# A gated mix of windowed attention and a GLU on one core: copies moved behind exponentials, three edits to the start

## The chip, the cores and the metric

The kernel runs on one core of one Trainium2 chip. The metric is the device time of one execution in microseconds, as the median of several runs, compared between the kernel before and the kernel after the change.

## The reference

Everything is float32, for one sequence of 2048 tokens with 512 features. Branch A is attention with 32 heads of 16 features, where each query sees itself and the 255 keys before it. Branch B is a gated linear unit with 1376 hidden features. A sigmoid gate for each token mixes them.

```python
g = sigmoid((x * gate_w).sum(-1, keepdims=True))
# A: qkv = x @ wqkv; scores = q k^T * 16**-0.5, masked to 0 <= i - j < 256; softmax; @ v; @ wo
# B: h = sigmoid(x @ w_gate) * (x @ w_up); h @ w_down
return g * a + (1 - g) * b
```

## The kernel before

Precision. TensorE is fed with a reduced 32-bit type. Each operand of a projection is therefore kept as two parts: a high part, made by a cast on ScalarE, and a low part, the difference from the original, made on VectorE (`lower`, `split`). A product is three matmuls: high times high, high times low, low times high.

Order. Apart from GpSimd, every engine's instruction order is the order in which the Python code issues the instructions (line 83). An engine that waits for something holds up all that stands behind it on the same engine.

The start. After fourteen warm-up matmuls on a cleared tile (lines 213 to 221) the loop at line 226 loads, for each of the four blocks d of 128 input features, the value weights and the first 512 tokens of x, both on SyncE's queue. ScalarE casts the weights and x, VectorE makes the low parts. For the first block alone, x is cast in two halves of 256 tokens: the first half by VectorE, the second by ScalarE. The matmuls that use them are those of lines 564 to 573 (`vps`): four token blocks, each in a bank of PSUM, over the four d. For the first d they run half by half, for the others all four token blocks together.

The long stretch. Attention runs over NU = 128 units u, one for each group of four heads (8 groups) and block of 128 tokens (16 blocks), with four heads hh in a unit. One pass of the inner loop, a slot, issues the scores of unit u for the maxima (`s_part`, line 372, TensorE and then a reduction on VectorE) and the transposed scores of unit u - 9 with their exponential (`st_part`, line 440; the exponential is line 454, on ScalarE). Both have two banks of PSUM each. Every eight units, at a wide visit, the products with v are taken (`pv_wide`).

The fill. Behind each slot the generator `turns` issues matmuls of the gate and up projections and of later query and key projections. How many steps follow a slot is written out in GAPS2 (first cycle) and GAPS3 (all others): lists of 31 sizes for the 32 slots of a cycle of eight units, the slot before a visit having none. A step is a pair of matmuls, one on each half of TensorE's rows. Three groups of 12 steps (for each half) share three banks. When a group is complete its copy out of PSUM, `gu_post` (line 633) or `proj_raw` (line 307), both on ScalarE, is put on the list `evac`.

Where a copy is issued. From line 1012: if u lies in the long stretch (`long`, from unit 9 to unit 120) and the slot is not the last one before a visit, a pending copy is issued ahead of the slot's scores, and so ahead of its exponential on ScalarE (`early`). Outside that stretch it is issued behind them (line 1035). Casts for later weights (`acts`, line 1037) are issued behind the scores too, when no copy was. Low parts and the like, on VectorE, come from the list `behind`.

The place of a slot in its cycle is k8 = (u - 9) % 8 * 4 + hh, from 0 to 31. The gap in front of it is GAPS3[k8 - 1]. GAPS3 has the value 2 at 1, 2, 4, 8 to 10, 21 to 23 and 28 to 30, the value 6 at 0, and 3 elsewhere.

Of the kernel before, what the change touches and what calls it, by code (L numbers as in the profile page):

```python
# [7 lines left out]
F32 = mybir.dt.float32  # L8
# [6 lines left out]
P = 128  # L15
# [6 lines left out]
HG = 4  # L22
# [18 lines left out]
LAG = 9  # L41
PVLAG = LAG + 4
WIDE = 2 * 4
# [6 lines left out]
GAPS3 = [6, 2, 2, 3, 2] + GAPS2[5:]  # L50
# [19 lines left out]
def gated_mix_kernel(  # L70
# [11 lines left out]
    nc = tc.nc  # L82
# [42 lines left out]
    NU = NG * NB  # L125
# [22 lines left out]
    with ExitStack() as actx:  # L148
# [45 lines left out]
        wvraw = Vf[:, 0:ND * D].rearrange("p (d n) -> p d n", d=ND)  # L194
# [3 lines left out]
        wv_v = wv.rearrange("(c p) n -> p c n", p=P)  # L198
# [12 lines left out]
            return dst, fill_d[v:v + 1].partition_broadcast(8).rearrange("(a j) o f -> a j (o f)", j=2)  # L211

        warm = cpool.tile([P, CH2], F32R, tag="hb", name="warm", bufs=2)
        nc.vector.memset(warm[:, 0:2 * P].bitcast(F32), 0.0)
        warm_ps = ps.tile([P, CH], F32, tag="st", name="warm_ps", bufs=2)

        def idle_mm(n):
# [5 lines left out]
        def lower(lo, src, hi):  # L223
            nc.vector.tensor_tensor(lo, src, hi.bitcast(F32), op=ALU.subtract)

        for d in range(ND):
            nc.sync.dma_start(wvraw[:, d], wv_v[:, d])
            nc.sync.dma_start(xraw[:, 0, d], xT[0, d])
            nc.scalar.copy(wvh[:, d], wvraw[:, d])
            if d:  # L230
                lower(wvl[:, d], wvraw[:, d], wvh[:, d])
            for h in range(2) if d == 0 else (None,):
                ts = slice(0, CH) if h is None else slice(h * CH // 2, (h + 1) * CH // 2)
                (nc.vector.tensor_copy if h == 0 else nc.scalar.copy)(xh[:, d, ts], xraw[:, 0, d, ts])
                if h == 0:
                    lower(wvl[:, 0], wvraw[:, 0], wvh[:, 0])
                lower(xl[:, d, ts], xraw[:, 0, d, ts], xh[:, d, ts])
        raw_q = [load_wqk(g) for g in range(2)]
# [115 lines left out]
        def run_dmas(dmas):  # L354
            for dst, src in dmas:
                nc.sync.dma_start(dst, src)
# [48 lines left out]
        def max_store(s):  # L405
            nc.sync.dma_start(max_d[s].rearrange("a h l b t -> (a h l b) t"), nms.pop(s))
# [66 lines left out]
        evac = []  # L473
# [89 lines left out]
              for b, (t, n) in enumerate((("s", 2), ("s", 2), ("st", 2), ("misc", 3)))]  # L563
        for d in range(ND):
            for w, bb in (
                [(w, (2 * h, 2 * h + 1)) for h in range(2) for w in range(3)] if d == 0
                else [(w, range(4)) for w in range(3)] if d < ND - 1 else [(None, range(4))]
            ):
                for b in bb:
                    bs = slice(b * P, (b + 1) * P)  # L570
                    for v in range(3) if w is None else (w,):
                        mm(vq[b], (xl if v == 2 else xh)[:, d, bs], (wvl if v == 1 else wvh)[:, d],  # L572
                           start=d == 0 and v == 0, stop=d == ND - 1 and v == 2)
# [51 lines left out]
        def gu_mm(f, c, w, k, half=None, second=False):  # L625
            if (f, c, w) not in gp:
                assert (f, w) in ready, (f, c, w)
                gp[f, c, w] = ps.tile([P, CH], F32, tag="misc", name=f"gu{f}_{c}_{w}", bufs=3)
            return group_mm(gp[f, c, w], gv[:, 0, w], gv[:, 1, w], c, k, half, second)
# [89 lines left out]
        def proj_slot(s, k, half):  # L719
            g, c = divmod(s, NC)  # L720
            d, w = divmod(k, 2) if k < 2 * ND else (k - 2 * ND, 2)
            r = slice(64 * half, 64 * half + 64)
            mm(pair_of_banks(f"ph{s}")[half], wq[g][int(w == 2)][r, d], (xl if w == 1 else xh)[r, d, c * CH:(c + 1) * CH],
               start=k == 0, stop=k == 3 * ND - 1)

        def proj_sum(s):
            lower, upper = halves.pop(f"ph{s}")
            t = cpool.tile([P, CH], F32, tag="sp", name=f"psum{s}", bufs=5)
            nc.scalar.copy(t, lower)
            pj[s] = t  # L730
            behind.append(lambda: nc.vector.tensor_tensor(t, upper, t, op=ALU.add))
            soon.append(lambda: proj_post(s))
# [6 lines left out]
                lambda k, h=None, x=False, a=(f, c, w): gu_mm(*a, k, h, x),  # L739
# [68 lines left out]
        def flush(acts):  # L808
            while acts:
                acts.pop(0)()  # L810
# [92 lines left out]
        def mid(u):  # L903
            return PVLAG <= u < NU and (u - PVLAG) % 4 == 0 and u not in visits

        U_WIDE = NB * NWIDE + LAG
        visits = {u: 2 for u in range(PVLAG + 4, U_WIDE + 1, WIDE)}
# [6 lines left out]
        for u in range(N):  # L914
# [48 lines left out]
            for s4 in proj_at.get(u, ()):  # L963
                if u < LAG:
                    first.insert(0, (
                        lambda k, h, s4=s4: proj_slot(s4, k, h), lambda s4=s4: proj_sum(s4)))
# [4 lines left out]
            for hh in range(HG):  # L971
                wide = visits.get(u) == 2
                if hh == 0 and u in visits:
                    s2 = (u - PVLAG) // 4 - wide
                    if wide:
                        banks = [[pv], []]
                        for n, tag in ((0, "st"), (1, "st"), (1, "s")):
                            banks[n].append(ps.tile([P, CH], F32, tag=tag, name=f"pv{s2}_{tag}{n}", bufs=2))
                        pv_wide(s2, banks)
                    else:  # L980
                        pv_part(s2, pv)
                if hh == 3 and mid(u + 1):
                    max_split((u - 4) // 4)
                if hh == 0 and mark:
                    if not mid(u):
                        max_split((u - 5) // 4)
                    run_dmas(later)
                    later.clear()
                    max_store((u - 5) // 4)
                if hh == 0 and wide:  # L990
                    flush(evac)
                    ripe = [held.pop(0) for _ in range(2) if held and held[0] // 2 == u // 8 + 1]
                    for s4 in ripe:
                        proj_hi(s4)
                    max_load((u - 5) // 4)
                    for s4 in ripe:
                        proj_lo(s4)
                    run_dmas(later)
                    later.clear()
                    for guests, n in ((acts, 2), (behind, 2 - len(ripe))):  # L1000
                        for _ in range(min(n, len(guests))):
                            guests.pop(0)()
                    o_sum(s2, 0, banks[0])
                    if behind:
                        behind.pop(0)()
                    o_sum(s2, 1, banks[1])
                    o_store(s2)
                elif hh == 0 and u in visits:
                    evac.append(lambda s2=s2: o_take(s2, pv))
                if hh == 2 and mark:  # L1010
                    transfers()
                long = LAG <= u < U_WIDE
                early = long and len(evac) > 0 and (hh < HG - 1 or u + 1 not in visits)
                if early:
                    evac.pop(0)()
                pair = [lambda: s_part(u, hh)] if u < NU else []
                if 0 <= u - LAG < NU:
                    pair.append(lambda: st_part(u - LAG, hh ^ 1 if u < NU else hh))
                for part in pair[::-1] if u % NB < 2 else pair:
                    part()  # L1020
                if u < LAG:
                    flush(behind)
                    if hh % 2 == 1:
                        upto = n_first * (2 * u + 1 + hh // 2) // (2 * LAG)
                        run_first(upto - done)
                        done = upto
                else:
                    k8 = (u - LAG) % WIDE * HG + hh
                    dense = GAPS2[max(0, k8 - 1)] < 3 if long else u < NU and (u - PVLAG) % 4 == 3 and hh > 0
                    k = (u - PVLAG) % 4 * HG + hh  # L1030
                    free = hh == 2 and not mid(u + 1) if long else k in (1, 5, 9) or k in (3, 7) and len(behind) > 2
                    guest = behind and (u < PVLAG or u >= NU or free)
                    if guest:
                        behind.pop(0)()
                    if evac and not long and not (u < NU and (guest or hh == 3 and mid(u + 1))):
                        evac.pop(0)()
                    elif acts and not early and not dense and (u < NU or hh % 2 == 1):
                        acts.pop(0)()
                if u >= LAG and (hh % 2 == 1 or u < NU) and (u + 1 not in visits or hh < HG - 1):
                    if u < N - 2:  # L1040
                        next(slots)
# [207 lines left out]
```

## Time and profile before

| | |
|---|---|
| median of three runs | 712.52 us (711.7 to 712.6) |
| the profiled execution | 711.69 us |
| its span, first to last instruction | 710.0 us |
| TensorE matmul busy | 705.3 us, 7542 matmuls |
| VectorE busy | 495.2 us |
| ScalarE busy | 435.3 us |
| GpSimd busy | 171.9 us |

The profile is of one execution. Times are in microseconds from the start of the span. A row of a view in order of time merges instructions of one kind that follow one another on their engine: the first number is the start of the first, the second the time to the end of the last, the number behind the x how many there are. In brackets stand the engine's idle time before the row and what ended it. PE is TensorE's matmuls, PEld its weight loads, DVE is VectorE, ACT ScalarE, POOL GpSimd, SP SyncE; a q behind the name is the engine's sequencer. The ends of matmuls are modelled, so distances between starts are the better measure of TensorE's pace.

### The profile page before, as it was taken

What the parts mean: (1) busy time and instruction counts of PE and PEld (TensorE: products, weight loads), DVE (VectorE), ACT (ScalarE), POOL (GpSimd) and SP (SyncE); (2) the same over time, 40 slices, a digit from 0 to 9 for tenths busy, and PEclk for the clock granted to TensorE, in tenths of its full rate; (3) what the DMA queues carried; (4) which work ended last, traced back from release to release, by engine and by line L of the source; (5) the groups of instructions that cost most, each with busy time, mean ns of one, the idle gap of its engine ahead of it and who ended that gap; (6) DMA issues with size and microseconds to landing.
All of it is one profiled execution on the core that took longest, in us unless ns stands there. A gap on an engine that the chain in (4) does not pass through costs nothing.

```text
span 710.0 us, 20054 instructions
## 1 busy us (share of the span) xinstructions
PE 705.3 (99%) x7542; PEld 626.6 (88%) x7542; DVE 495.2 (70%) x1484; ACT 435.3 (61%) x889; POOL 171.9 (24%) x254
## 2 busy tenths in 40 slices
PE   9999999999999999999999999999999999999998
PEld 7888889999899998999889989999888888888886
DVE  5368767767777776776777777777747858667481
ACT  6423777677676677767767767765676735435341
POOL 5200333233233233323323323333341000000000
PEclk9999999999999999999999999999999999999999
DMA  8466644636446264573645627664579859778521
GB/s 307 115 196 195 216 162 145 218 126 210 155 168 229 79 231 157 164 226 114 200 152 186 213 80 214 209 210 112 179 202 289 268 141 244 168 187 241 149 62 60
DMA packets 102832, 127.38 MB, mean 179 GB/s; under 512 B 45750, under 2 KB 62390, under 8 KB 102736
## 3 DMA queue, kind: packets, MB, share of 16 engines
q1 hardware_dynamic: 102592, 125.98, 58.0%
q8 instruction: 59, 0.97, 0.6%
q14 instruction: 37, 0.30, 0.1%
q10 hardware_dynamic: 144, 0.13, 0.1%
HBM read 71.80 MB, written 51.13 MB: 173 GB/s over the span
## 4 chain that ended last, share of the span: by engine, by line
PE 99%; DVE 0%; issue 0%; DVEq 0%
PE gu L294 28%; PE pj L294 13%; PE st L447 6%; PE s L382 6%; PE tp L673 6%; PE pd L100 5%; PE pd L98 5%; PE pd L99 5%; PE pv_st L502 4%; PE vh L710 4%; PE pv_s L502 3%; PE pa L98 2%; PE pa L99 2%; PE pa L100 2%; PE pv L502 2%; PE vps L572 2%
## 5 line engine op out<-in xcount | busy, mean ns | idle before, releaser
L388 DVE CUSTOM_DVE_ANT_0 junk<-s,mask 128x384 f32<-128x384 f32 (+2 forms) x512 | 271.3, 530 | 93.0 <-PE s L382 39.7
L294 PE MATMUL gu<-xh,w 64*128 64x512 f32 x1152 | 270.8, 392 | 0.0
L454 ACT ACTIVATE pbuf<-st 128x384 f32<-128x384 f32 (+2 forms) x344 | 164.3, 490 | 59.7 <-PE st L447 26.5
L294 PE MATMUL gu<-xl,w 64*128 64x512 f32 x576 | 186.1, 389 | 0.0
L447 PE MATMUL st<-ring 64*128 64x384 f32 (+2 forms) x536 | 167.0, 328 | 0.0
L382 PE MATMUL s<-ring 64*128 64x384 f32 (+2 forms) x536 | 163.9, 324 | 0.1
L294 PEld LDWEIGHTS gu<-xh,w 64*128 64x128 f32 x1152 | 159.7, 184 | 4.0
L461 POOL TENSOR_SCALAR_AFFINE_SELECT pbuf<-pbuf 128x512 f32<-128x512 f32 x86 | 58.1, 676 | 276.1 <-ACT pbuf L454 266.9
L382 PEld LDWEIGHTS s<-ring 64*128 64x128 f32 x536 | 94.9, 184 | 10.7 <-DVE mx L388 2.6
L447 PEld LDWEIGHTS st<-ring 64*128 64x128 f32 x536 | 95.7, 184 | 8.2 <-ACT V L454 2.1
L294 PEld LDWEIGHTS gu<-xl,w 64*128 64x128 f32 x576 | 92.0, 184 | 1.2
L454 ACT ACTIVATE V<-st 128x384 f32<-128x384 f32 (+2 forms) x168 | 72.5, 440 | 29.9 <-PE s L382 17.8
L294 PE MATMUL pj<-xl,wqh 64*128 64x512 f32 (+1 forms) x228 | 80.5, 389 | 0.0
L294 PE MATMUL pj<-xh,wqh 64*128 64x512 f32 (+1 forms) x228 | 80.3, 389 | 0.0
L294 PE MATMUL pj<-xh,wql 64*128 64x512 f32 (+1 forms) x228 | 69.7, 389 | 0.0
L99 PE MATMUL pd<-ring,hb 128*128 128x512 f32 x160 | 62.3, 389 | 0.0
L98 PE MATMUL pd<-ring,hb 128*128 128x512 f32 x160 | 62.3, 389 | 0.0
L100 PE MATMUL pd<-ring,hb 128*128 128x512 f32 x160 | 62.3, 389 | 0.0
L94 ACT CAST hb<-V 128x512 fp32r<-128x512 f32 x40 | 24.9, 622 | 60.1 <-DVE V L873 46.5
L467 POOL TENSOR_SCALAR_AFFINE_SELECT pbuf<-pbuf 128x512 f32<-128x512 f32 x84 | 56.0, 666 | 0.0
L633 ACT COPY sp<-gu 128x512 f32<-128x512 f32 x72 | 42.3, 587 | 13.7 <-PE gu L294 8.9
L461 POOL TENSOR_SCALAR_AFFINE_SELECT V<-V 128x512 f32<-128x512 f32 x42 | 28.0, 667 | 71.2 <-ACT V L454 50.1
(155 smaller groups left out, 1372.1 us busy)
## 6 DMA issues: line engine op xcount, KB each, us to landing
gu_scratch<-sp SPq DMA_DIRECT2D x72, 256.0 KB
V<-gu_scratch SPq DMA_DIRECT2D x36, 512.0 KB
ring<-stack_scratch SPq DMA_DIRECT2D x56, 256.0 KB
stack_scratch<-sh SPq DMA_DIRECT2D x14, 512.0 KB
stack_scratch<-sl SPq DMA_DIRECT2D x14, 512.0 KB
ring<-stack_scratch SPq DMA_DIRECT2D x14, 512.0 KB
guraw<-in_wgu_dram SPq DMA_DIRECT2D x18, 256.0 KB
v_scratch<-V SPq DMA_DIRECT2D x4, 1088.0 KB
```

The costliest lines, as they stand in the source:

```text
L98: mm(ps, lh, rh, start=first, stop=False)
L99: mm(ps, lh, rl, start=False, stop=False)
L100: mm(ps, ll, rh, start=False, stop=last)
L294: return mm(pt, (wl if w == 2 else wh)[r, d], (xl if w == 1 else xh)[r, d, c * CH:(c + 1) * CH], start=k == 0 and not second, stop=k == 3 ...
L382: mm(pt[:, (k - k0) * P:(e - k0) * P], lhsT, blk(g, k, hh, 1, e - k), start=k == k0, stop=e == i + 1, skip_group_check=True,)
L388: nc.vector.tensor_tensor_reduce(junk[:, 0:n], pt[:, 0:n], mask[:, 3 * P - n:], scale=1.0, scalar=NEG, op0=ALU.add, op1=ALU.max, accum_out ...
L447: mm(pt[:, (q - j) * P:(e - j) * P], lhsT, blk(g, q, hh, 0, e - q), start=q == j, stop=e == last, skip_group_check=True,)
L454: exps.append(nc.scalar.activation(out, pt[:, 0:n * P].rearrange(seen, t=HB, **({} if len(out.shape) == 3 else {"k": 2})), AF.Exp, scale=S ...
L461: nc.gpsimd.affine_select(buf[:, s0:s0 + 2], buf[:, s0:s0 + 2], pattern=[[HB, 2], [0, HG], [1, HB]], compare_op=ALU.is_ge, fill=0.0, base= ...
L467: nc.gpsimd.affine_select(old, old, pattern=[[-HB, 2], [0, HG], [-1, HB]], compare_op=ALU.is_gt, fill=0.0, base=0, channel_multiplier=1,)
L502: mm(bank[32 * hh:32 * hh + w, o + k * HB:o + e * HB], vt[HB * half:HB * half + HB, v:v + w], p_run(g * NB + j, hh, half, k, e), start=fir ...
L673: return mm(tp[b][:, 0:TW], (xl if w == 1 else xh)[r, d, b * P:(b + 1) * P], tw[d][int(w == 2)][r, 0:TW], start=k == 0 and not second, sto ...
```

## The change

Four things are altered.

- The zeros for the warm-up matmuls: VectorE clears the first 128 of the 256 columns and GpSimd the others.
- The first block of the value weights is loaded by a DMA that is issued on ScalarE's queue; all other loads stay on SyncE's.
- The second block of x (d = 1) is also cast in two halves, the first by VectorE and the second by ScalarE, and its matmuls run half by half like those of the first.
- In the long stretch a pending copy is issued behind the slot's scores and exponential, and no longer ahead of them, where k8 is over 8 and the gap in front of the slot has fewer than three steps (`tight`). The test that no copy is issued in the last slot before a visit now holds for the stretch behind as well.

```diff
         warm = cpool.tile([P, CH2], F32R, tag="hb", name="warm", bufs=2)
-        nc.vector.memset(warm[:, 0:2 * P].bitcast(F32), 0.0)
+        nc.vector.memset(warm[:, 0:P].bitcast(F32), 0.0)
+        nc.gpsimd.memset(warm[:, P:2 * P].bitcast(F32), 0.0)
...
         for d in range(ND):
-            nc.sync.dma_start(wvraw[:, d], wv_v[:, d])
+            (nc.sync if d else nc.scalar).dma_start(wvraw[:, d], wv_v[:, d])
             nc.sync.dma_start(xraw[:, 0, d], xT[0, d])
...
-            for h in range(2) if d == 0 else (None,):
+            for h in range(2) if d < 2 else (None,):
...
-                if h == 0:
+                if h == 0 and d == 0:
                     lower(wvl[:, 0], wvraw[:, 0], wvh[:, 0])
...
-                [(w, (2 * h, 2 * h + 1)) for h in range(2) for w in range(3)] if d == 0
+                [(w, (2 * h, 2 * h + 1)) for h in range(2) for w in range(3)] if d < 2
...
                 long = LAG <= u < U_WIDE
-                early = long and len(evac) > 0 and (hh < HG - 1 or u + 1 not in visits)
+                k8 = (u - LAG) % WIDE * HG + hh
+                tight = long and k8 > 8 and GAPS3[k8 - 1] < 3
+                last = hh == HG - 1 and u + 1 in visits
+                early = long and len(evac) > 0 and not last and not tight
...
-                    if evac and not long and not (u < NU and (guest or hh == 3 and mid(u + 1))):
+                    if evac and not last and (tight if long else not (u < NU and (guest or hh == 3 and mid(u + 1)))):
                         evac.pop(0)()
```

## Rows read from the trace of the kernel before

**Rows 1.** The page: its first line, and TensorE's busy time, share and instructions.

```profile
span 710.0 us, 20054 instructions
PE   705.3 (99%) x7542; PEld 626.6 (88%) x7542; DVE 495.2 (70%) x1484; ACT 435.3 (61%) x889; POOL 171.9 (24%) x254
```

**Rows 2.** All waits of TensorE's matmuls: us in total, times, longest.

```profile
PE warm_ps L219 <- DVE warm L214: 1.3, 1, 1.3
```

**Rows 3.** In order of time, the first 9 us, all engines (columns as described above).

```profile
0.80 0.42 POOL L247 MEMSET mask<- 128x384 f32 x1 [0.29 <-POOLq L1236]
0.81 0.39 SPq L227 DMA_DIRECT2D V<-in_wv_dram  x1
0.93 0.27 DVE L214 MEMSET warm<- 128x256 f32 x1 [0.93 <-PEq L1236]
...
1.25 3.36 PE L219 MATMUL warm_ps<-warm 128*128 128x256 f32 x14 [1.25 <-DVE warm L214]
1.26 0.41 SPq L228 DMA_DIRECT2D V<-in_xT_dram  x1
...
3.44 0.62 ACT L229 CAST w<-V 128x512 fp32r<-128x512 f32 x1 [1.36 <-DMA V<-in_wv_dram]
...
4.08 0.41 ACT L234 CAST xh<-V 128x256 fp32r<-128x256 f32 x1
4.08 0.29 DVE L234 CAST xh<-V 128x256 fp32r<-128x256 f32 x1 [2.89 <-DMA V<-in_xT_dram]
...
4.50 0.50 PEld L572 LDWEIGHTS vps<-w,xh 128*128 128x128 f32 x2 [0.18 <-ACT xh L234]
...
4.90 0.75 DVE L224 TENSOR_TENSOR xl<-V,xh 128x256 fp32r<-128x256 f32 x2
...
6.94 0.62 ACT L234 CAST xh<-V 128x512 fp32r<-128x512 f32 x1 [1.38 <-DMA V<-in_xT_dram]
...
7.19 0.62 PE L572 MATMUL vps<-w,xl 128*128 128x512 f32 x2
...
7.61 0.76 PEld L572 LDWEIGHTS vps<-w,xh 128*128 128x128 f32 x4 [0.23 <-ACT xh L234]
7.64 1.17 PE L572 MATMUL vps<-w,xh 128*128 128x512 f32 x4
...
8.65 1.08 PE L572 MATMUL vps<-wvl,xh 128*128 128x512 f32 x4
```

**Rows 4.** In order of time, the last microseconds: the one DMA on ScalarE's queue.

```profile
707.20 0.37 ACTq L1197 DMA_DIRECT2D out_dram<-spare  x1
```

**Rows 5.** In order of time, TensorE's matmuls around a copy at k8 = 11.

```profile
106.95 0.33 PE L447 MATMUL st<-ring 64*128 64x384 f32 x1
...
108.68 0.33 PE L447 MATMUL st<-ring 64*128 64x384 f32 x1
...
108.86 0.39 PE L294 MATMUL gu<-xh,w 64*128 64x512 f32 x1
```

**Rows 6.** In order of time, ScalarE at the same place.

```profile
106.80 0.49 ACT L454 ACTIVATE pbuf<-st 128x384 f32<-128x384 f32 x1 [0.15 <-PE st L447]
107.31 0.59 ACT L633 COPY sp<-gu 128x512 f32<-128x512 f32 x1
107.79 1.06 ACT L454 ACTIVATE pbuf<-st 128x384 f32<-128x384 f32 x2
```

**Rows 7.** Waits of TensorE's weight loads from 73 to 485 us: total, times, longest.

```profile
PEld st L447 <- ACT V L454: 2.1, 7, 0.3
...
PEld st L447 <- ACT pbuf L454: 1.4, 5, 0.3
```

**Rows 8.** In order of time: two of these 12 waits, and ScalarE at the second.

```profile
93.03 0.18 PEld L447 LDWEIGHTS st<-ring 64*128 64x128 f32 x1 [0.33 <-ACT V L454]
...
443.24 0.18 PEld L447 LDWEIGHTS st<-ring 64*128 64x128 f32 x1 [0.27 <-ACT V L454]
...
443.26 0.59 ACT L633 COPY sp<-gu 128x512 f32<-128x512 f32 x1
```

More of the change, by code (lines that the diff above doesn't have):

```diff
@@ L1027, in gated_mix_kernel @@
                 else:
-                    k8 = (u - LAG) % WIDE * HG + hh
                     dense = GAPS2[max(0, k8 - 1)] < 3 if long else u < NU and (u - PVLAG) % 4 == 3 and hh > 0
```

## The prediction

> **What bounds the kernel now.** I read the page first: TensorE is busy for 705.3 of the 710.0 us of the span [rows 1]. That alone does not prove that it is the bound, since the ends of matmuls are modelled, so the list of TensorE's waits came next: in the whole run it holds a single one, 1.3 us before the first warm-up matmul [rows 2]. From there to the last output matmul one matmul follows another. So an edit pays only if it shortens that stream: by letting real matmuls start earlier, or by removing a gap between two of them. A copy or a cast that merely moves on another engine pays nothing. The views to read are therefore the first 9 us in order of time (what the first matmuls wait for) and the waits of the weight loads in the long attention stretch (what opens gaps there). The profiled execution took 711.69 us, 0.83 us below the median of the three runs (712.52); the sum is made against 711.69 and the same difference is applied to the median.
>
> **Zeros cleared by two engines.** VectorE clears 256 columns in 0.27 us (from 0.93), and the warm-up matmuls start at 1.25, 0.05 us after it [rows 3]. Half of that is 0.13 us. GpSimd clears 384 columns in 0.42 us from 0.80 [rows 3], so its 128 columns, which now stand ahead of the mask, take about 0.14 and are done by 0.95, before VectorE is. The warm-up starts and ends 0.13 us earlier. That is worth nothing by itself, because the first real weight load already waits 0.18 us beyond the warm-up [rows 3]: it only raises the possible gain at that place to 0.31. GpSimd's later work slips 0.14 us; none of it releases TensorE here.
>
> **First weights on ScalarE's queue.** Today SyncE issues the weights at 0.81 and x at 1.26; the casts show them landed at 3.44 and 4.08 [rows 3]. ScalarE casts the weights until 4.06, VectorE casts the first half of x until 4.37, and the first real weight load starts at 4.50, 0.13 later [rows 3]. With the change both issue at about 0.8. ScalarE's issue costs some 0.37 us, by the one that this kernel has on that queue [rows 4]; it is covered by the 1.36 us for which ScalarE is idle ahead of its first cast [rows 3]. All that SyncE issues after it is issued 0.45 us earlier. What it brings hangs on when the two land. Best: the weights as now, x no later than 3.75. Then the weights' cast (end 4.06) decides and the load can start at 4.19: gain 0.31, just the room that the warm-up leaves. Worst: the two share the transfer and both land at 4.08. Then the weights' cast runs from 4.08 to 4.70 (0.62), the load starts at 4.83, and 0.33 is lost. No row has two queues active at the start, so both ends stay in the range. The distance of the two landings, 0.64, is larger than that of the issues, 0.45: the transfer and not the issue is the limit, which points to the middle. I take 0 for the first load.
>
> The Trainium skill, page "DMA: Bandwidth & Descriptors", section "Issuing engines are not separate DMA queues", says that transfers from different issuing engines run on the same 16 engines and interleave, and that several issuers save only issue time. By that rule the best case is not to be had and the worst is the likelier end; the 0.64 against 0.45 agrees with it as far as it goes.
>
> **Second x block in halves.** Its cast by ScalarE starts at 6.94 when it lands, takes 0.62, and the weight load starts at 7.61 after an idle 0.23 [rows 3]. That 0.23 is not what it costs. The pair of matmuls before it starts at 7.19, two take 0.45, so the next was due at 7.64 at the earliest, and started at 7.64 [rows 3]. The loss shows only in the next four, 1.01 us from 7.64 to 8.65 where four at that pace take 0.91: 0.10 us. Halving the cast (VectorE's half takes 0.29, by the same form at 4.08) lets the load start near 6.94 + 0.29 + 0.13 = 7.36, so the 0.10 goes; nothing else does while the matmuls before it end where they do. If the start gained 0.31 above, the matmuls are ready at 7.33, and the halves let nearly all of that through; without them the landing at 6.94 would have eaten it. VectorE has room for the 0.29: it waits for ScalarE there. The reordered matmuls of that block need the low part of the first half four matmuls (0.9 us) after the load, and VectorE makes two such halves in 0.75 [rows 3], so it is in time. Taken: -0.10, with ends -0.41 and +0.23 for the whole start.
>
> **Copies behind exponentials.** In the long stretch a copy of a finished group now stands before its slot's exponential; the change puts it behind where the gap in front of the slot has two matmul pairs and the slot's place in its cycle of 32 (k8) is over 8. By the copies' places in the trace that is 20 of them: ten at k8 = 11 and ten at k8 = 24. What follows at these two places is a gap of three pairs. One of the ten shows the pattern: the copy runs at 107.31 and delays its exponential to 107.79, where it could have started near 107.35, after the one before it began at 106.80 and its scores, from 106.95, were through [rows 5, 6]. The delay is 0.4 us. But the scores that wait for that exponential's bank stand two slots on, at 108.68 [rows 5], and it is done at 108.28: 0.4 us to spare, 0.2 if its weight load is taken off. Is there any place where it bites? In the 412 us of the stretch, weight loads of that line wait for an exponential 12 times, 3.5 us in all, the longest 0.3 [rows 7]. By their times, five stand at the short gaps ahead of the wide visits, behind copies at k8 = 28, such as the 0.33 at 93.03 [rows 8]; the gap in front of k8 = 28 has three pairs, so those copies are not moved. Four stand right behind those visits, at k8 = 3. The last three lie near a moved copy, and each ends before that copy starts: the one at 443.24 precedes the copy at 443.26 [rows 8]. So nothing that the trace shows is removed: gain 0. As a bound I keep those three idle stretches: at 0.27 each, some 0.7 us.
>
> What it adds: the copy ends about 0.5 us later (exponential from 107.35 to 107.84, copy to 108.43 instead of 107.89), and the PSUM bank that it empties is due to the next group. In the pattern that group's first matmul starts at 108.86 [rows 5], so some 0.2 us of room is left when its weight load, 0.2 ahead, is taken off. The next exponential is not delayed either: two of them take 1.06 from 107.79 [rows 6], so it starts near 108.36 today, and the copy fits in front of that. Taken: 0. The tests for the last slot before a visit change the late stretch only if a copy is pending there; in the trace none is.
>
> **Sum.** Start -0.10, copies 0, and a little (-0.1) for the earlier issue of all later loads, the middle between nothing and half of the best case: 711.69 - 0.2 = 711.5 for an execution like the profiled one, 712.3 as a median. The whole shift at the start passes to the end, since the stream has no other wait.
>
> **Rivals.** (1) The weights land late, as the worst case above: the first load at 4.83, +0.33, against -0.10 of the halves: +0.2, so 712.7. Page rule and landing distance speak for it, chance 0.25; it is still within the measurement. (2) The copies do matter, through delays too short to be listed as waits: 20 exponentials start 0.4 us earlier, and if a quarter of that reached TensorE it would be 2.0 us: 710.3. Against it: the 0.2 to 0.4 us to spare in the pattern. Chance 0.08. (3) Slower: the emptied bank comes too late. It decides from the point where the copy ends over 0.2 us after 108.43 in the pattern; if each of the 20 then held the next group for 0.1 us, it is +2.0, 714.3. For it: the room is the smallest of all that I computed. Against it: no other ScalarE work stands between these exponentials. Chance 0.07. (4) The change does not do what it says at the short gaps, because those copies are followed by long ones: that is my forecast for this part.
>
> **How the numbers follow.** The forecast (a gain of 0 to 0.5 us) has 0.60, the rivals 0.25, 0.08 and 0.07. A difference under 0.2% (1.4 us), about what a measurement of this kernel can tell from no change, is all that the forecast and rival 1 give. Faster takes rival 2 and a little of the forecast's tail with the best case at the start and the 0.7 of the copies: 0.12. Slower is rival 3: 0.07. Same: 0.81. The range: 712.5 less 0.4 (start) less 0.7 (copies) gives 711.4, and the three runs spread over 0.9 us, so low 711.0; above, +0.23 and half that spread give 713.2.
>
> **What would show it.** In the changed profile: the warm-up starts near 1.12; the first real weight load lies between 4.19 and 4.83, which tells the landing cases apart; the four matmuls of the second block take 0.91, not 1.01; at 20 places an exponential precedes the copy, and the following matmuls keep their distances. I am wrong if weight loads of the new groups wait for a copy, if the waits for exponentials lose more than those three, or if the span moves by more than the shift of the first 10 us.

## The result, and the profile after

| | before | after |
|---|---|---|
| median, lowest to highest | 712.21 us (711.2 to 713.2), 17 executions | 713.93 us (712.1 to 715.4), 17 executions |
| ratio after to before | | 1.0022, 95% interval 1.0015 to 1.0030 |
| profiled execution | 711.69 us, span 710.0 | 715.03 us, span 713.3 |

The change makes the kernel slower by 1.7 us. The forecast was 712.3 (711.0 to 713.2) with 0.07 on slower: wrong in size and in sign. The profiled execution of after is one of its longer ones, 1.1 us above the median, which matters below where single terms are read from it.

The page's first line and TensorE's row, which answer to [rows 1]:

```profile
span 713.3 us, 20053 instructions
PE 708.1 (99%) x7542; PEld 627.6 (88%) x7542; DVE 495.4 (69%) x1486; ACT 433.8 (61%) x889; POOL 172.2 (24%) x255
```

The same 7542 matmuls are now busy for 708.1 us, 2.8 more: the matmuls themselves have become longer somewhere. All waits of TensorE's matmuls (us in total, times, longest), to set against [rows 2]:

```profile
PE warm_ps L220 <- DVE warm L214: 1.2, 1, 1.2
PE vps L573 <- ACT w L230: 0.8, 1, 0.8
```

A second wait has come up, ahead of the first real matmul, and it names the cast of the weights. The start in order of time (columns as in [rows 3]):

```profile
0.80 0.41 ACTq L228 DMA_DIRECT2D V<-in_wv_dram  x1
...
0.80 0.39 SPq L229 DMA_DIRECT2D V<-in_xT_dram  x1
0.90 0.17 DVE L214 MEMSET warm<- 128x128 f32 x1 [0.90 <-PEq L1239]
...
1.21 3.33 PE L220 MATMUL warm_ps<-warm 128*128 128x256 f32 x14 [1.21 <-DVE warm L214]
...
4.43 0.29 DVE L235 CAST xh<-V 128x256 fp32r<-128x256 f32 x1 [3.37 <-DMA V<-in_xT_dram]
...
4.65 0.62 ACT L230 CAST w<-V 128x512 fp32r<-128x512 f32 x1 [2.13 <-DMA V<-in_wv_dram]
...
5.32 0.50 PEld L573 LDWEIGHTS vps<-w,xh 128*128 128x128 f32 x2 [1.08 <-ACT w L230]
5.32 1.22 PE L573 MATMUL vps<-w,xh 128*128 128x512 f32 x2 [0.79 <-ACT w L230]
...
6.34 1.05 PE L573 MATMUL vps<-wvl,xh 128*128 128x512 f32 x2
6.58 0.68 DVE L225 TENSOR_TENSOR wvl<-V,w 128x512 fp32r<-128x512 f32 x1
6.59 0.41 ACT L235 CAST xh<-V 128x256 fp32r<-128x256 f32 x1 [0.49 <-DMA V<-in_xT_dram]
...
7.18 0.29 DVE L235 CAST xh<-V 128x256 fp32r<-128x256 f32 x1
7.19 1.05 PE L573 MATMUL vps<-w,xl 128*128 128x512 f32 x2
...
8.90 1.05 PE L573 MATMUL vps<-wvl,xh 128*128 128x512 f32 x2
...
10.36 0.63 PE L573 MATMUL vps<-w,xh 128*128 128x512 f32 x2
```

Two things are to be seen. By the starts of their casts, the weights are there at 4.65 (before: 3.44) and x at 4.43 (before: 4.08), so the first real weight load starts at 5.32 in place of 4.50, after 1.08 us of idle time. And from there the matmuls go at another pace: a pair starts every 0.85 us, 0.427 for a matmul of 512 columns, which is the lower of TensorE's two levels (512 columns at 1.2 GHz). In the kernel before the pairs from 5.37 on stood 0.45 apart, near the upper one:

```profile
5.37 0.62 PE L572 MATMUL vps<-wvl,xh 128*128 128x512 f32 x2
...
5.83 0.62 PE L572 MATMUL vps<-w,xl 128*128 128x512 f32 x2
```

The fourteen warm-up matmuls, of 256 columns each, start 0.213 apart behind the first, which is the lower level, in both kernels. Before, the rise comes among the first real matmuls; after, it comes at 10.1 us. The 13th real matmul starts at 10.36, before it started at 7.64: of this 2.72 the late start of the first is 0.79, and the pace behind it 1.93.

The profile's own clock column does not show this. One stretch of the start, first before, then after. Behind the length of the stretch stand the busy times of PE, PEld, DVE, ACT and POOL, each with the number of its instructions, then the granted clock as a share of the upper level, the busy share of the DMA engines and the GB/s that they moved:

```profile
5.00:10.00 5.00, 5.00 (x22) 3.91 (x21) 3.69 (x7) 3.48 (x6) 0.00 (x0) 1.00 1.02 359
```

```profile
5.00:10.00 5.00, 4.68 (x11) 3.67 (x12) 4.66 (x11) 4.14 (x9) 0.00 (x0) 1.00 1.01 370
```

The granted clock stands at 1.00 in both rows, but 11 matmuls pass in 5 us where 22 passed before. The column gives 1.00 for time of which the trace has no record of the clock. The first record, of the upper level, begins at 5.18 us before and at 10.06 after, which is where the distances of the starts change. So it is the clock that rises later.

Behind the start little differs. The waits of the weight loads from 76 to 488 us, against [rows 7]:

```profile
PEld st L448 <- ACT V L455: 2.1, 7, 0.3
...
PEld st L448 <- ACT pbuf L455: 1.5, 5, 0.3
```

And the pattern of [rows 5, 6], 2.64 us later, with its copy behind the exponential:

```profile
110.11 0.49 ACT L455 ACTIVATE pbuf<-st 128x384 f32<-128x384 f32 x1 [0.19 <-PE s L383]
...
110.50 0.58 ACT L634 COPY sp<-gu 128x512 f32<-128x512 f32 x1
...
110.99 0.49 ACT L455 ACTIVATE pbuf<-st 128x384 f32<-128x384 f32 x1
...
111.49 0.39 PE L295 MATMUL gu<-xh,w 64*128 64x512 f32 x1
```

The copy ends at 111.08 (forecast: 108.43 + 2.64 = 111.07), and the next group's first matmul at 111.49 is where 108.86 + 2.64 puts it: no delay. In this profile the offset to before grows from 2.64 at 117 us to 3.6 at 258 us and stays between 3.4 and 3.8 from there on. That last microsecond was the one reason left to suspect the copies.

### The profile page after: what moved, and what is told of

It reads as the page before. It is cut to its first block, busy times and chain, and to the rows that moved or that the text cites. A ratio compares the mean times of both kernels' runs of the same rounds, so it can differ in the third digit from the quotient of the medians.

```text
span 713.3 us, 20053 instructions
## 1 busy us (share of the span) xinstructions
PE 708.1 (99%) x7542; PEld 627.6 (88%) x7542; DVE 495.4 (69%) x1486; ACT 433.8 (61%) x889; POOL 172.2 (24%) x255
## 4 chain that ended last, share of the span: by engine, by line
PE 99%; DMA 1%; ACT 0%; DVE 0%; issue 0%
PE gu L295 28%; PE pj L295 13%; PE st L448 6%; PE s L383 6%; PE tp L674 6%; PE pd L99 5%; PE pd L100 5%; PE pd L98 5%; PE pv_st L503 4%; PE vh L711 4%; PE pv_s L503 3%; PE pa L98 2%; PE pa L99 2%; PE pa L100 2%; PE vps L573 2%; PE pv L503 2%
```

## The experiments

Theory A: the whole loss is at the start, late landings and with them a later rise of the pace. Theory B: the moved copies, in the long stretch. The kernel before was timed anew beside each group; its median is given with each result.

**The change without the other queue.**

```diff
-            (nc.sync if d else nc.scalar).dma_start(wvraw[:, d], wv_v[:, d])
+            nc.sync.dma_start(wvraw[:, d], wv_v[:, d])
```

> The changed kernel with the first weights issued on SyncE's queue again; the split zeros, the halves of the second x block and the moved copies stay. Theory A (the loss is the start: the weights land late, TensorE falls idle and then runs at half pace for longer): the first weight load is back near 4.5 us, the first twelve real matmuls are at full pace from about 5.3 us, and the time is that of the kernel before, 712.2 within 0.4. Theory B (the loss is the moved copies in the long stretch): still 713.5 to 714.

Measured: 712.55 us, before 712.25, ratio 1.0003 (0.9992 to 1.0013). The loss is gone with the queue. The profiled execution is its longest, 715.03 us; in that one x came late on the single queue:

```profile
3.57 0.62 ACT L230 CAST w<-V 128x512 fp32r<-128x512 f32 x1 [1.49 <-DMA V<-in_wv_dram]
...
4.80 0.41 ACT L235 CAST xh<-V 128x256 fp32r<-128x256 f32 x1 [0.61 <-DMA V<-in_xT_dram]
...
5.21 0.50 PEld L573 LDWEIGHTS vps<-w,xh 128*128 128x128 f32 x2 [0.97 <-ACT xh L235]
```

An idle 0.97 us ahead of the first load, and again the lower pace until 10.1 us. So the event isn't bound to two queues; they make it common.

**The other queue alone, in the kernel before.**

```diff
-            nc.sync.dma_start(wvraw[:, d], wv_v[:, d])
+            (nc.sync if d else nc.scalar).dma_start(wvraw[:, d], wv_v[:, d])
```

> The kernel before with one edit: the first weights issued on ScalarE's queue. Theory A: as slow as the changed kernel, 713.5 to 714.2; the first weight cast starts near 4.6 us in place of 3.4, the first real weight load near 5.3. Theory B: 712.2, no change.

Measured: 714.33, before 712.25, ratio 1.0024 (1.0015 to 1.0033), the whole loss of the change. In its profile the landings are later still:

```profile
5.08 0.29 DVE L234 CAST xh<-V 128x256 fp32r<-128x256 f32 x1 [3.89 <-DMA V<-in_xT_dram]
5.30 0.62 ACT L229 CAST w<-V 128x512 fp32r<-128x512 f32 x1 [2.79 <-DMA V<-in_wv_dram]
...
5.97 0.50 PEld L572 LDWEIGHTS vps<-w,xh 128*128 128x128 f32 x2 [1.66 <-ACT w L229]
```

**The copies alone.** The hunk of the change from `k8` to `evac.pop(0)()`, in the kernel before, and nothing else.

```diff
-                early = long and len(evac) > 0 and (hh < HG - 1 or u + 1 not in visits)
+                early = long and len(evac) > 0 and not last and not tight
```

> The kernel before with the moved copies alone. Theory A: 712.2 within 0.4, and the same slot lengths behind the 20 moved copies. Theory B: 713 or more, with weight loads of new groups waiting for a copy.

Measured: 711.96, before 712.25, ratio 0.9995 (0.9986 to 1.0003): no difference that shows, and surely not +1.7. Theory B falls. The last microsecond in the profile of after isn't the copies either: two kernels below that hold the same moved copies, after with 20 warm-ups and the change without the halves, end without such a growth in their profiles (offsets of 1.16 and 2.31 at 117 us, 1.09 and 2.38 at the end), while the one without the other queue has it (2.59 and 3.42). Where it comes from stays open.

**The pace by itself.** Four warm-up matmuls fewer leave TensorE idle ahead of data that land as before.

```diff
-        idle_mm(14)
+        idle_mm(10)
```

> The kernel before with 10 warm-up matmuls in place of 14; nothing else. The first real matmuls cannot start earlier or later than before, as their data land as before; only TensorE's idle time ahead of them grows from 0.2 to about 1.1 us. Theory A with the pace as its larger part: half pace lasts longer, up to twelve matmuls more at 0.2 us each, 713 to 714.5 in the median, though the first weight load stays at 4.5. If the idle time does not matter to the pace and the landing alone costs: 712.2.

Measured: 713.82, before 712.25, ratio 1.0017 (1.0009 to 1.0026). The rows of the start:

```profile
3.46 0.62 ACT L229 CAST w<-V 128x512 fp32r<-128x512 f32 x1 [1.38 <-DMA V<-in_wv_dram]
...
4.16 0.29 DVE L234 CAST xh<-V 128x256 fp32r<-128x256 f32 x1 [2.96 <-DMA V<-in_xT_dram]
...
4.57 0.50 PEld L572 LDWEIGHTS vps<-w,xh 128*128 128x128 f32 x2 [1.11 <-ACT xh L234]
...
5.59 1.05 PE L572 MATMUL vps<-wvl,xh 128*128 128x512 f32 x2
...
6.44 1.05 PE L572 MATMUL vps<-w,xl 128*128 128x512 f32 x2
...
9.77 1.09 PE L572 MATMUL vps<-w,xh 128*128 128x512 f32 x4
```

The data land at 3.46 and 4.16 and the first load starts at 4.57, 0.07 later than before; only the idle time ahead of it is 1.11 in place of 0.18. The pairs then stand 0.85 apart, and the 13th real matmul starts at 9.77, 2.13 later than before. An idle stretch that delays nothing by itself costs 1.6 us through the pace.

**The late data without the loss of pace.** In the kernel after:

```diff
-        idle_mm(14)
+        idle_mm(20)
```

> The kernel after with 20 warm-up matmuls instead of 14; nothing else changed. Twenty at the 0.22 to 0.24 us that the trace of before shows for one end near 5.5 us, past the 5.32 at which the first real weight load started in the profile of after. Theory A (most of the loss is the pace: TensorE stands idle ahead of its first real matmuls and then goes through them at 0.427 instead of 0.227 us each): no or little idle time ahead of the first real matmul, the real ones at 0.227 to 0.235 from the first or nearly so, and only the later start is lost, about 0.8 us: 712.7 to 713.1. Rival A' (the landing of the data is the whole loss, each later block is late too): the time stays at 713.7 to 714.2 although the pace is full.

Measured: 712.98, before 712.28, ratio 1.0011 (1.0002 to 1.0020): 0.95 us less than after. Its profile has x at 4.93 and the weights at 5.16, later than in that of after, and yet:

```profile
1.21 4.14 PE L220 MATMUL warm_ps<-warm 128*128 128x256 f32 x20 [1.21 <-DVE warm L214]
...
5.83 0.30 PEld L573 LDWEIGHTS vps<-w,xh 128*128 128x128 f32 x2 [0.68 <-ACT w L230]
...
7.12 0.62 PE L573 MATMUL vps<-w,xl 128*128 128x512 f32 x2
...
7.58 0.62 PE L573 MATMUL vps<-w,xh 128*128 128x512 f32 x2
```

The pairs stand 0.46 apart. The rise came within the warm-up: its last four distances are 0.11 to 0.17 where the others are 0.213, and the record of the upper level begins at 4.64. The warm-up still ended short of the data, but the idle time behind the rise, 0.68 ahead of the first load, did not take the pace back. What is left is the late start: 0.7 us in the medians, 1.3 at the 13th matmul of this profile.

**The two loads exchanged.** In the kernel before, x on ScalarE's queue and the weights on SyncE's, as they were.

```diff
-            nc.sync.dma_start(xraw[:, 0, d], xT[0, d])
+            (nc.sync if d else nc.scalar).dma_start(xraw[:, 0, d], xT[0, d])
```

> The kernel before with the first block of x loaded from ScalarE's queue and the weights on SyncE's: the two are exchanged against the change. Theory A1 (two loads that are issued at once on two queues share the transfer, and both land late): the cast of the weights on ScalarE starts at 4.3 us or later instead of 3.44, x lands between 4.3 and 5.2, the first real load starts at 4.9 to 6.0 and the time is 713.7 to 714.5, as with the weights on that queue. Rival A2 (it is ScalarE's queue that is slow or late to begin, SyncE's is as before): the weights land at 3.4, x alone is late, at 4.4 to 5.2; the first load follows x by 0.4 us. Rival A3 (only the weights' lateness counted): both land by 4.1 and the time is 712.2 or less.

Measured: 713.92, before 712.28, ratio 1.0022 (1.0013 to 1.0031).

```profile
4.42 0.62 ACT L229 CAST w<-V 128x512 fp32r<-128x512 f32 x1 [1.90 <-DMA V<-in_wv_dram]
...
4.66 0.29 DVE L234 CAST xh<-V 128x256 fp32r<-128x256 f32 x1 [3.46 <-DMA V<-in_xT_dram]
```

The weights, issued from the same queue at the same time as before, land 0.98 us later: ScalarE's queue isn't slow by itself, the two loads delay each other (A1). The transfer in the stretch from 2.4 to 3.0 us (the last number is GB/s), in the kernels before, after, and this one:

```profile
2.40:3.00 0.60, 0.60 (x5) 0.60 (x4) 0.00 (x0) 0.00 (x0) 0.54 (x3) 1.00 0.98 355
```

```profile
2.40:3.00 0.60, 0.60 (x5) 0.60 (x4) 0.00 (x0) 0.12 (x1) 0.54 (x3) 1.00 0.42 164
```

```profile
2.40:3.00 0.60, 0.60 (x5) 0.60 (x4) 0.00 (x0) 0.12 (x1) 0.54 (x3) 1.00 0.49 184
```

Not only do the loads share: from 2.4 to 3.0 us both queues together move about half of what the single queue moved, so even the one that ends last ends later than before. In all five profiles with two queues it is 143 to 184 GB/s in this stretch, in the nine with one 290 to 389. The two loads aren't alone either: SyncE's queue had moved 536 KB when the weights were cast in after, and x is 256 of them; the rest belongs to the loads behind x, which are now issued earlier. Why the rate falls is not in the trace. ScalarE's table load also starts later in these kernels, at 1.23 or 1.24 in place of 0.80, because it stands behind the issue, and no run parts this from the second queue.

**A reserve of three warm-up matmuls, in the kernel before.**

```diff
-        idle_mm(14)
+        idle_mm(17)
```

> The kernel before with 17 warm-up matmuls instead of 14. Theory A: in the kernel before the warm-up ends close to the first real load, so three more only cover the executions in which the data lands a little late: the same median within 0.3 us or up to 0.5 lower, 711.7 to 712.4, and a narrower spread. Rival (the pace depends on the idle time hardly at all, ten were slow for another reason, such as the number of warm-up matmuls itself): a step from 10 to 14 of 1.6 us goes on, and 17 give 711.0 or less. Rival (the warm-up only takes time): 3 x 0.23 less the idle 0.18 gives +0.5, 712.7.

Measured: 712.11, before 712.28, ratio 0.9998 (0.9989 to 1.0007), all executions between 711.2 and 712.6. As theory A expects: they cost nothing that shows, and the step of 1.6 us between ten and fourteen doesn't go on.

**Other copies moved.** Those at k8 = 8 and 28 in place of 11 and 24, in the kernel before: the same hunk as for the copies alone, but with

```diff
+                tight = long and k8 in (8, 28)
```

> The kernel before with the copies at k8 = 8 and k8 = 28 behind the exponentials, and none moved at 11 or 24. These are the places ahead of short gaps on both sides; behind copies at k8 = 28 stood five of the twelve waits of weight loads for an exponential in the trace of before, 0.3 us each. If the copies delay an exponential that TensorE then waits for: these five waits are gone, up to 1.3 us less, 710.9 to 711.6. If those waits are ended by something that is late anyway (the scores' own place behind a short gap): 712.0 to 712.4, with the five waits still there. Slower, if the emptied bank comes late to the next group: 713 or more, with waits of new groups' weight loads for a copy.

Measured: 711.87, before 712.28, ratio 0.9996 (0.9987 to 1.0004). Two of the five waits in question, first before, then here:

```profile
270.45 0.18 PEld L447 LDWEIGHTS st<-ring 64*128 64x128 f32 x1 [0.34 <-ACT V L454]
...
329.69 0.18 PEld L447 LDWEIGHTS st<-ring 64*128 64x128 f32 x1 [0.29 <-ACT V L454]
```

```profile
270.61 0.18 PEld L447 LDWEIGHTS st<-ring 64*128 64x128 f32 x1 [0.19 <-ACT V L454]
...
330.22 0.18 PEld L447 LDWEIGHTS st<-ring 64*128 64x128 f32 x1 [0.16 <-ACT V L454]
```

The five shrink from about 0.31 to 0.19 each, 0.6 us in all, and don't go. That is of the size of the 0.4 in the medians, which by itself doesn't show.

**The halves alone, in the kernel before**, and **the change without the halves**; the second edit is the first one reversed in the kernel after.

```diff
-            for h in range(2) if d == 0 else (None,):
+            for h in range(2) if d < 2 else (None,):
...
-                [(w, (2 * h, 2 * h + 1)) for h in range(2) for w in range(3)] if d == 0
+                [(w, (2 * h, 2 * h + 1)) for h in range(2) for w in range(3)] if d < 2
```

> The kernel before with the second x block cast in halves and its matmuls run half by half; the queues, the zeros and the copies as before. By the sum of the prediction: -0.10, since the idle 0.23 us ahead of that block's load cost 0.10: 712.0 to 712.3, a difference that these rounds hardly show. Theory A agrees: nothing lies between the warm-up and the first real matmul that this edit touches. Rival (the halves themselves cost time, because the high and low parts of half a block come later than the matmuls want them): a wait ahead of the second block's matmuls for xl, and 712.6 or more.

> The kernel after with the second x block cast in one piece again and its matmuls in the order of before; queue, zeros and copies stay changed. If the halves cost time of their own (alone they gave 712.79 against 712.05, ratio 1.0009): 713.0 to 713.4. If they are worth the -0.1 of the prediction or nothing, and the 0.7 was the chance of late landings in those executions: 713.8 to 714.3, as after.

Measured: alone 712.79, before 712.05, ratio 1.0009 (1.0001 to 1.0018). Taken from the change: 713.88, before 712.33, ratio 1.0021, against 1.0022 with them. The two don't agree. The profiled execution of the first (713.46 us) had x at 4.47, 0.57 idle ahead of the first load, two matmuls' distances at the lower pace, and one wait that no other profile of these has in this size:

```profile
PE st L447 <- DMA ring<-max_scratch: 0.9, 1, 0.9
```

None of that touches the halves, and with their removal gaining nothing twice (here and in the last run), I read the 0.7 as late landings in those eleven executions. This is argued; the run was not made again.

**The harmless parts together**, in the kernel after: weights on SyncE's queue, and

```diff
-        idle_mm(14)
+        idle_mm(17)
...
-                tight = long and k8 > 8 and GAPS3[k8 - 1] < 3
+                tight = long and (k8 in (8, 28) or k8 > 8 and GAPS3[k8 - 1] < 3)
```

then the same without the halves.

> The kernel after with three edits: the first weights back on SyncE's queue, 17 warm-up matmuls instead of 14, and the copies behind the exponentials at k8 = 8 and 28 too. If the parts that cost nothing or a little less by themselves (copies at 11 and 24: 0.9995, copies at 8 and 28: 0.9996, 17 warm-ups: 0.9998, halves: about -0.1 us) add up: 0.9988 or so, 711.4 to 711.7. If they were chance: 712.0 to 712.4, as before. If more than four copies in a cycle behind the exponentials hold up the banks: 712.8 or more, with waits of the groups' weight loads for a copy.

> The combination (weights on SyncE's queue, 17 warm-ups, two engines for the zeros, copies at k8 = 8, 11, 24 and 28 behind the exponentials) without the halves of the second x block. If the halves cost time of their own: 710.6 to 711.1. If they are worth nothing or -0.1: 711.4 to 711.8, as with them (711.49). Whether the combination as such is faster than before is tried a second time with it: 0.9991 again, or 1.0000 if that was chance.

Measured: 711.49 with the halves (before 712.05, ratio 0.9991, 0.9982 to 1.0000) and 711.55 without (before 712.33, ratio 0.9988, 0.9979 to 0.9996). The singles of copies (0.9995, 0.9996) and warm-ups (0.9998) multiply to 0.9989, so they seem to add up, some 0.7 us, which no part shows by itself. Twice this kernel lies below before, but the first interval reaches 1.0000. The start of the second:

```profile
4.25 0.29 DVE L235 CAST xh<-V 128x256 fp32r<-128x256 f32 x1 [3.19 <-DMA V<-in_xT_dram]
...
4.76 0.55 PEld L573 LDWEIGHTS vps<-w,xh 128*128 128x128 f32 x2
4.97 1.06 PE L573 MATMUL vps<-w,xh 128*128 128x512 f32 x2
...
5.82 1.05 PE L573 MATMUL vps<-wvl,xh 128*128 128x512 f32 x2
...
7.47 0.63 PE L573 MATMUL vps<-w,xh 128*128 128x512 f32 x2
```

No idle time ahead of the load, and still the first matmuls stand 0.427 apart in this execution, five distances in all, where the profile of before has none.

All profiles side by side, in the order in which the clock rose (one execution each; x and weights: starts of the first casts; first real load and the idle time ahead of it; rise: where the trace's record of the upper level begins; low: distances of 0.42 to 0.44 us among the first 30 real matmuls, from their starts; the time of this execution; the median of all):

| kernel | x | weights | first load | idle | rise | low | this one | median |
|---|---|---|---|---|---|---|---|---|
| copies alone | 4.16 | 3.53 | 4.57 | 0.25 | 4.29 | 0 | 711.7 | 712.0 |
| after, 20 warm-ups | 4.93 | 5.16 | 5.83 | 0.68 | 4.64 | 0 | 712.6 | 713.0 |
| copies at 8 and 28 | 4.43 | 3.42 | 4.84 | 0.53 | 4.73 | 0 | 711.9 | 711.9 |
| before | 4.08 | 3.44 | 4.50 | 0.18 | 5.18 | 0 | 711.7 | 712.2 |
| 17 warm-ups | 4.12 | 3.54 | 4.83 | 0 | 5.40 | 0 | 711.6 | 712.1 |
| halves alone | 4.47 | 3.53 | 4.88 | 0.57 | 6.65 | 2 | 713.5 | 712.8 |
| harmless parts | 4.47 | 3.54 | 4.88 | 0 | 7.02 | 3 | 712.0 | 711.5 |
| the same without halves | 4.25 | 3.48 | 4.76 | 0 | 7.39 | 5 | 712.4 | 711.6 |
| weights on ScalarE's queue alone | 5.08 | 5.30 | 5.97 | 1.66 | 9.50 | 6 | 714.1 | 714.3 |
| ten warm-ups | 4.16 | 3.46 | 4.57 | 1.11 | 9.64 | 10 | 714.2 | 713.8 |
| the change without the halves | 4.25 | 4.47 | 5.14 | 0.90 | 9.69 | 9 | 713.9 | 713.9 |
| x on ScalarE's queue | 4.66 | 4.42 | 5.09 | 0.78 | 9.73 | 9 | 714.4 | 713.9 |
| after | 4.43 | 4.65 | 5.32 | 1.08 | 10.06 | 9 | 715.0 | 713.9 |
| the change without the other queue | 4.80 | 3.57 | 5.21 | 0.97 | 10.06 | 10 | 715.0 | 712.6 |

In the six profiles with 0.78 us of idle time or more the clock rises at 9.5 to 10.1 us, in the other eight at 4.3 to 7.4. The number of warm-up matmuls doesn't part the two groups, since fourteen stand in both. Late data don't either, since ten warm-ups had them on time and after with 20 had them late. So the idle time ahead of the rise makes a late rise the rule. What spreads it from 4.3 to 7.4 in the others, three of them without any idle time, is not shown.

## Why the prediction was wrong

**Zeros.** The warm-up started 0.04 earlier (1.21), not 0.13. Worth nothing as said; with the late data it only lengthens the idle time.

**First weights on ScalarE's queue: the step that failed, twice.** Its worst end let the two loads share the transfer and land at the time at which x alone had landed, 4.08. That took the sum of both transfers as fixed. The runs show the pair landing at 4.43 and 4.65, 4.66 and 4.42, 5.08 and 5.30: the worst end of +0.33 should have been +0.6 to +1.5 by the first loads at 5.09 to 5.97. The landing term measures 0.7 us (the kernel with 20 warm-ups against before, with the other parts of the change in it). The -0.1 for the earlier issue of all later loads was a guess between nothing and half of the best case, and the packets point the other way: these loads took a share of the transfer that the first matmul waited for. The Trainium skill, page "DMA: Bandwidth & Descriptors", section "Issuing engines are not separate DMA queues", had pointed to this end with its rule that such transfers interleave. The exchange of the loads agrees with that; that the rate falls to 164 from 355 GB/s for 0.6 us goes beyond the rule.

The larger miss is a term that the sum did not hold. It put the shift of the first load through to the end one to one ("the whole shift at the start passes to the end"), with the matmuls behind it at the pace of before. But the warm-up is there so that the pace rises by the time the real work comes; in the profiles with a hole of 0.78 to 1.66 us ahead of the rise, it came at 9.5 us or later. Ten warm-ups, with the data on time, price that at 1.6 us. In after the two terms give 1.7 in the medians and not 2.3; presumably not each execution has the long hole (they spread from 712.1 to 715.4), but only one was profiled. The rows of before would have allowed a warning: fourteen warm-up matmuls of 256 columns in 3.36 us and pairs of 512 columns 0.45 apart [rows 3] are two paces, and the prediction did not ask what the change from one to the other hangs on.

**Halves.** The 0.10 is real only where the start is as early as before: from the 13th to the 25th real matmul before takes 2.85 us, the copies alone 2.80, and all other profiles take 2.72 to 2.76 with or without the halves. In the change they are worth nothing. That VectorE "has room for the 0.29" held only in the profile of before, where this block of x landed last, at 6.94. In after VectorE's half starts at 7.18, 0.59 behind ScalarE's, because the weights' low part stands ahead of it (6.58); in the halves alone it is 6.55 against 5.92.

**Copies.** Right: 0, with 20 copies moved, the times of the copy and of the next group met to 0.01 us (the exponential came 0.12 later than forecast), and no group's weight load waiting for a copy. The bound of 0.7 was not reached; rivals 2 and 3 fell with the copies alone (711.96).

**Rivals.** Rival 1 named the mechanism (the weights land late) and gave it 0.25, but priced it at +0.2, "still within the measurement". With the terms now measured it is +1.7, outside it. No rival held that an idle TensorE goes on at the lower pace; the one forecast of slower stood on the copies.

## What to carry to other kernels

Price a late first operand as the delay plus what TensorE's pace loses if the hole opens ahead of the rise; here the second was the larger. Size the warm-up for the latest landing of the data and not for the usual one: here three matmuls too many cost nothing that shows, four too few cost 1.6 us, and six more in the changed kernel gave back 0.95. Two loads that the first matmul needs together did not come earlier here by being issued on two queues at once; one after the other, the first can be cast while the second moves.

## What the runs showed of the hardware

- Two loads of 256 KB issued at 0.8 us on two queues: both queues together moved 143 to 184 GB/s from 2.4 to 3.0 us (five profiles), where one queue moved 290 to 389 (nine profiles). The weights were there at 4.42 to 5.30 us instead of 3.42 to 3.57, x at 4.25 to 5.08 instead of 4.08 to 4.80.
- TensorE took 0.427 us for 512 columns, six to ten times in a row, after idle stretches of 0.78 to 1.66 us behind fourteen or ten warm-ups whose pace had not risen yet. After 0.68 us behind twenty, the last of which ran faster, no distance was that long and they settled at 0.227.
- The granted clock reads 1.00 where the trace has no record of it; the first record, and the change in the distances, came at 4.3 to 10.1 us.
- With one queue, the landing of x varied between executions from 4.08 to 4.80 us.
